# A chunked RWKV-7 recurrence and a GELU MLP in one kernel: the MLP moved one chunk later, and the start reordered

## The chip, the core and the metric

The kernel runs on one core of one Trainium2 chip. The metric is the device time of a whole execution in microseconds (us). TensorE (PE) multiplies matrices out of SBUF into PSUM; VectorE (DVE), ScalarE (ACT) and GpSimd (POOL) do the elementwise work; SyncE (SP) issues most transfers. Each engine runs its own instructions in the order in which the program lists them, and waits on semaphores for the others. PSUM holds four tiles of the kind `duo`, which is all that TensorE writes to.

## What is computed

Two stages: a linear recurrence with a state of 40 x 40 for each of 4 x 8 heads over 768 steps, and an MLP with exact GELU on its output.

```python
batch, n_heads, seq, head_dim = (4, 8, 768, 40)     # r, k, v, w, a, b: float32
n_tokens, d_model, d_ff = (3072, 320, 2048)         # moe_w_in, moe_w_out: float64
for t in range(S):
    y[:, :, t] = np.einsum('bhd,bhde->bhe', rt, state)
    Sa = np.einsum('bhde,bhe->bhd', state, at)
    state_decay = state * wt[:, :, None, :] - np.einsum('bhd,bhe->bhde', Sa, bt)
    state = state_decay + np.einsum('bhd,bhe->bhde', vt, kt)
x = y.transpose(0, 2, 1, 3).reshape(B * S, H * D)
h = x @ w_in
out = (0.5 * h * (1.0 + erf(h * inv_sqrt2))) @ w_out
```

The two weights come as float64. [...]

## The kernel before, in words

The sequence is cut into 12 chunks of 64 steps. Inside a chunk the recurrence becomes matrix products; only the state goes from chunk to chunk. For a chunk c these are the steps, each a function (names of tiles as in the profile):

- `sums(c)`: logarithm of `w_raw` on ScalarE, running sums `cum` on TensorE, exponentials on ScalarE. `turns_a(c)`: scaling by them (`nb` on VectorE, `ks` on GpSimd) and transposes to `wT`, `aT`, `nT`. `turns_b(c)`: transposes to `kT`, `vT`, `rT`.
- `make_N(c)`: the products `N` of a head's steps with each other, and their 32 x 32 blocks to DRAM (`N<-N`).
- `invert(c)`: the blocks come back with one block in each partition (`Nb<-N`), and 31 columns, two instructions each, invert the unit triangular blocks into `W`. VectorE does it for chunk 0, GpSimd for all others.
- `fetch_inverse(c)`: `W` to DRAM (`inv<-W`) and back as a matrix (`Tt<-inv`, `T2`). `corner(c)` transposes it on VectorE (`L`) and multiplies (`J`); `joined(c)` adds the missing quarter (`J2`, the second `J` of the profile).
- `make_RV`, `make_A`, `make_av`, `make_X`, `make_sa`, `make_saT`, `make_M`, `make_y2`, `make_QY`: the products that lead to the output and the new state. `X` needs the state of the chunk before, `sap` needs `Tt`, and `QY` comes last.
- `outputs(c)`: VectorE makes `xt` (the MLP's input) and the new state `st` out of `QY`. Parts of `xt` then move between partitions by ten small transfers, `xt<-xt`, five issued by SyncE and five by ScalarE.
- `mlp(c)`: a generator that yields after each piece: four pieces `ph` (`xt` by `w_in`, then GELU into `gt`) and four pieces `po` (`gt` by `w_out`), each a few us of TensorE. `os` takes the result out of PSUM, and SyncE writes it.

`fill()` emits the next piece of the oldest MLP that is queued. The loop over chunks emits, in iteration c, `make_N` and `invert` of chunk c+1, the state-dependent steps of chunk c with `fill()` in between, `outputs(c)`, and then queues `mlp(c)` and goes on with the other steps of chunks c+1 and c+2, with four more `fill()`. So the four `ph` pieces of chunk c follow its own `outputs(c)`, and the `po` pieces fall into iteration c+1.

The order on TensorE and SyncE is that of the code (`manual_schedule`); on VectorE, ScalarE and GpSimd a scheduler at build time chooses it. All of SyncE's transfers form one queue: one that waits holds those behind it. `a`, `v`, `r`, `xt`, `os`, `Nb`, `W`, `Tt` and `gt` have one buffer each.

The weights are converted (`to_float`, seven VectorE instructions for a tile) in the first two iterations: five tiles of `w_in` (`first_load`, `first_convert`), whose words pass through two halves of the unused `gt`, and sixteen tiles of `w_out` (`second_weights`), whose words pass through two buffers `wo_raw`.

Of the kernel before, what the change touches and what calls it, by code (L numbers as in the profile page):

```python
# [10 lines left out]
FP32 = mybir.dt.float32  # L11
# [5 lines left out]

HI_MIN = float(np.array(0x38100000, np.uint32).view(np.float32))
# [3 lines left out]
def kernel(  # L22
# [103 lines left out]
    def rows_of(src, c, g, e):  # L126
        return src[G * g + e, :, c * C:(c + 1) * C, :].rearrange("h t d -> t h d")

    def fetch(c, n, src, eng):
        t = work.tile([P, G, H, D], FP32, tag=n + "_raw", name=n + "_raw")  # L130
        for g in range(G):
            for e in range(2):
                eng.dma_start(out=t[half(e), g], in_=rows_of(src, c, g, e))  # L133
        raws[c, n] = t

    def fetch_padded(c, n, src, eng, placed):

        t = padded[n]()
        for g in range(G):
            for e in range(2):  # L140
                rows = rows_of(src, c, g, e)
                if placed:
                    for y in range(2):
                        eng.dma_start(out=t[half(e), g, y::2, :D], in_=rows[:, NP * y:NP * (y + 1)])  # L144
                else:
                    eng.dma_start(out=t[half(e), g, :, :D], in_=rows)
        raws[c, n] = t
# [7 lines left out]
    def load_kb(c):  # L155
        fetch(c, "k", k, nc.sync)
        fetch(c, "b", b, nc.sync)
# [7 lines left out]
    ctx.enter_context(tc.manual_schedule(engines={mybir.EngineType.PE, mybir.EngineType.SP}))  # L165
# [54 lines left out]
    def to_float(dst, words):  # L220


# [3 lines left out]
        top = work.tile([P, LW], UINT32, tag="top", name="top")[:, :n]  # L226
        low = work.tile([P, LW], UINT32, tag="low", name="low")[:, :n]
        nc.vector.tensor_scalar(low, hi, 3, 0x3FFFFFFF, ALU.logical_shift_left, ALU.bitwise_and)
        nc.vector.scalar_tensor_tensor(top, hi, 0xC0000000, low, ALU.bitwise_and, ALU.bitwise_or)
        top, low_f = top.bitcast(FP32), low.bitcast(FP32)  # L230
        nc.vector.tensor_scalar(low, hi, 0x7FFFFFFF, None, ALU.bitwise_and)
        nc.vector.scalar_tensor_tensor(top, low_f, HI_MIN, top, ALU.is_ge, ALU.mult)
        nc.vector.tensor_scalar(low, top.bitcast(UINT32), 0xFF800000, None, ALU.bitwise_and)
        nc.vector.scalar_tensor_tensor(low_f, lo, 2.0 ** -52, low_f, ALU.mult, ALU.mult)
        nc.vector.tensor_tensor(dst, top, low_f, ALU.add)  # L235

    first_raw, second_raw = {}, {}

    def first_load(kt):
# [10 lines left out]
    def first_convert(kt):  # L250
        if kt in first_raw:
            to_float(w_in_sb[:, kt], first_raw.pop(kt))

    def second_weights(lo_f, hi_f):
        wide = moe_w_out.dtype != FP32
        src = moe_w_out.bitcast(UINT32) if wide else moe_w_out
        for f in range(lo_f, hi_f):
            dst = w_out_sb[:, f]
            to = work.tile([P, 2 * DM], UINT32, tag="wo_raw", name="wo_raw", bufs=2) if wide else dst
            nc.sync.dma_start(out=to, in_=src[f * P:(f + 1) * P])  # L260
            if wide:
                to_float(dst, to)
# [50 lines left out]
    def turns_b(c):  # L313
        t = turned_in[c]
        kT = t["kT"] = side("kT", "kT", 1)
# [6 lines left out]
        nc.vector.tensor_copy(vT, flip(by_place(v_), "vT_ps"))  # L322
        rT = t["rT"] = side("rT", "rT", 2)
        nc.vector.tensor_copy(rT, flip(by_place(raws.pop((c, "r"))), "rT_ps"))
# [396 lines left out]
```

## Time and profile before

| | |
|---|---|
| median of 3 runs | 992.87 us (the runs: 991.69, 992.87, 995.45) |
| the profiled execution | 997.0 us, its span 995.3 us, mean granted TensorE clock 0.859 |
| busy: PE, PEld, DVE, ACT, POOL | 747.5, 609.4, 317.6, 236.5, 301.7 us |
| transfers | 60.41 MB in 255247 packets, mean 61 GB/s |
| in the first 50 us | 123 GB/s |

The span runs from the first to the last instruction. A row of the timeline gives start, length, engine, line, operation, output<-inputs, shapes, count, and in brackets the idle time ahead of it with what ended it. SPq and ACTq are the issues of transfers by SyncE and ScalarE. In a row of the groups the numbers behind the bar are busy us and mean ns of one instruction. TensorE takes a float32 product in two passes, so a count in the trace is twice that of the program.

### The profile page before, as it was taken

Reading aid. Unit: us, or ns where it says so; the run is one execution under the profiler, and the core shown is the slowest. Engines: PE = TensorE matmul, PEld = TensorE weight load, DVE = VectorE, ACT = ScalarE, POOL = GpSimd, SP = SyncE. Lnnn points to the kernel's source line nnn. Section 1 sums busy time; section 2 is a strip of 40 time slices with the busy share of each in tenths; the row PEclk is TensorE's granted clock in tenths of the full one; section 3 lists DMA queues with packets and bytes.
Section 4 is the critical chain, followed back from the end, with each engine's and each line's share of the span. In section 5 each row is a group of like instructions: output and inputs, shape, how many; then the busy total and the mean of one; then the engine's idle time right before and its main releaser. Section 6 shows DMA issues by size and latency. Waiting matters only on the chain.

```text
span 995.3 us, 29674 instructions
## 1 busy us (share of the span) xinstructions
PE 747.5 (75%) x13256; PEld 609.4 (61%) x13256; DVE 317.6 (32%) x479; ACT 236.5 (24%) x254; POOL 301.7 (30%) x777
## 2 busy tenths in 40 slices
PE   3433407667896994994995996995994996988978
PEld 2332406545774873874874874874874875867776
DVE  2771637783132132222231232221322322230110
ACT  2200013201511520520520611611511413302110
POOL 3008100008218118117036036036045054062000
PEclk9655658788898898997997997997997997998989
DMA  8624273345224134134143053043053053012000
GB/s 126 121 45 83 68 105 91 87 104 88 40 55 79 33 59 79 29 66 78 22 83 71 15 90 68 9 90 67 9 96 68 11 100 59 13 37 39 9 21 14
DMA packets 255247, 60.41 MB, mean 61 GB/s; under 512 B 241232, under 2 KB 250960, under 8 KB 255120
## 3 DMA queue, kind: packets, MB, share of 16 engines
q1 hardware_dynamic: 248864, 55.89, 30.6%
q10 hardware_dynamic: 6256, 2.63, 1.3%
q8 instruction: 104, 1.70, 0.7%
q14 instruction: 23, 0.19, 0.1%
HBM read 44.30 MB, written 10.22 MB: 55 GB/s over the span
## 4 chain that ended last, share of the span: by engine, by line
PE 64%; SPq 12%; DMA 10%; DVE 10%; issue 4%; POOL 0%; ACTq 0%; DVEq 0%; ACT 0%; POOLq 0%
PE ph L576 22%; PE po L583 19%; SPq L144 6%; DMA xt<-xt 3%; PE QY L98 2%; DMA out_dram<-os 2%; PE J L98 2%; SPq L133 2%; SPq L590 1%; PE saT_ps L98 1%; PE RV_ps L98 1%; PE cum L98 1%; PE A_ps L98 1%; PE M_ps L98 1%; PE kT_ps L284 1%
## 5 line engine op out<-in xcount | busy, mean ns | idle before, releaser
L576 PE MATMUL ph<-xt,w_in_sb 64*128 64x256 f32 x1920 | 246.5, 414 | 150.5 <-DMA xt<-xt 150.5
L576 PEld LDWEIGHTS ph<-xt,w_in_sb 64*128 64x128 f32 x1920 | 207.3, 207 | 182.4 <-issue 160.5
L583 PE MATMUL po<-w_out_sb,gt 128*128 128x320 f32 x768 | 224.7, 446 | 5.9 <-DVE w_out_sb L235 5.5
L398 POOL TENSOR_TENSOR tmp<-W,Nb 128x126 f32<-128x126 f32 (+22 forms) x341 | 125.1, 367 | 342.6 <-DMA Nb<-N 316.6
L583 PEld LDWEIGHTS po<-w_out_sb,gt 128*128 128x128 f32 x768 | 144.6, 193 | 65.6 <-DVE w_out_sb L235 6.5
L400 POOL TENSOR_TENSOR W<-W,tmp 128x126 f32<-128x126 f32 (+22 forms) x341 | 130.2, 382 | 26.7
L578 ACT ACTIVATE gt<-ph 128x1024 f32<-128x1024 f32 x48 | 49.2, 1024 | 187.9 <-PE ph L576 187.9
L578 ACT ACT_TABLE_LOAD x30 | 38.5, 1283 | 159.5 <-DMA xt<-xt 156.9
L304 POOL TENSOR_TENSOR ks<-k_raw,part 128x640 f32<-128x640 f32 x12 | 21.5, 1792 | 103.4 <-ACT part L276 103.4
L587 DVE COPY os<-po 128x320 f32<-128x320 f32 x24 | 11.8, 492 | 128.0 <-PE po L583 84.4
L494 ACT COPY saT<-saT_ps 128x512 f32<-128x512 f32 x12 | 7.0, 586 | 178.7 <-issue 157.6
L274 DVE COPY cs_pad<-cum 128x640 f32<-128x640 f32 x12 | 9.9, 823 | 114.7 <-PE cum L98 114.7
L533 DVE TENSOR_TENSOR y<-QY,y 128x512 f32<-128x512 f32 x22 | 15.1, 686 | 64.3 <-PE QY L98 64.3
L322 DVE COPY vT<-vT_ps 128x1024 f32<-128x1024 f32 x12 | 14.7, 1224 | 54.9 <-PE vT_ps L284 54.9
L98 PE MATMUL cum<-w_raw,cum_m 128*128 128x320 f32 x48 | 18.4, 512 | 16.6 <-ACT w_raw L269 16.6
L328 DVE TENSOR_TENSOR SM<-M_ps,upper 128x1024 f32<-128x1024 f32 x12 | 14.7, 1224 | 50.2 <-PE M_ps L98 50.2
L390 POOL MEMSET W<- 128x512 f32 x11 | 5.8, 529 | 82.0 <-DMA inv<-W 82.0
L328 DVE TENSOR_TENSOR VR<-RV_ps,upper 128x1024 f32<-128x1024 f32 x12 | 14.7, 1223 | 44.6 <-PE RV_ps L98 44.6
L455 DVE COPY Tt<-J 32x512 f32<-32x512 f32 x12 | 8.3, 689 | 59.4 <-ACT Tt L455 59.4
L284 PE MATMUL vT_ps<-ident,v_pad 128*128 128x128 f32 x96 | 14.5, 298 | 16.7 <-DMA v_pad<-in_v_dram 16.7
L308 DVE TENSOR_TENSOR aT<-aT_ps,wpT 128x1024 f32<-128x1024 f32 x12 | 14.7, 1224 | 33.7 <-ACT wpT L306 27.5
L269 ACT ACT_TABLE_LOAD x12 | 15.4, 1283 | 38.6 <-DMA w_raw<-in_w_dram 27.6
(110 smaller groups left out, 937.2 us busy)
## 6 DMA issues: line engine op xcount, KB each, us to landing
Nb<-N SPq DMA_DIRECT2D x24, 256.0 KB
wo_raw<-in_moe_w_out_dram SPq DMA_DIRECT2D x16, 320.0 KB
w_raw<-in_w_dram SPq DMA_DIRECT2D x48, 80.0 KB
k_raw<-in_k_dram SPq DMA_DIRECT2D x48, 80.0 KB
b_raw<-in_b_dram SPq DMA_DIRECT2D x48, 80.0 KB
r_pad<-in_r_dram SPq DMA_DIRECT2D x96, 40.0 KB
out_dram<-os SPq DMA_DIRECT2D x48, 80.0 KB
a_pad<-in_a_dram SPq DMA_DIRECT2D x44, 80.0 KB
```

Of the source, the lines that this page charges most:

```text
L98: nc.tensor.matmul(o, lhsT, rhs, start=first, stop=True, skip_group_check=True)
L133: eng.dma_start(out=t[half(e), g], in_=rows_of(src, c, g, e))
L144: eng.dma_start(out=t[half(e), g, y::2, :D], in_=rows[:, NP * y:NP * (y + 1)])
L269: nc.scalar.activation(logw, logw, ACT.Ln)
L284: nc.tensor.transpose(pt[:, g, n], src(g, n), ident)
L304: nc.gpsimd.tensor_tensor(ks[:, :, :, :D], raws.pop((c, "k")), rwv, ALU.mult)
L328: nc.vector.tensor_tensor(to, pt, upper.unsqueeze(1).to_broadcast([P, 2 * G * NP, C]), ALU.mult)
L398: eng.tensor_tensor(t, W[:, :rows, j:j + 1].to_broadcast([P, rows, rest]), Nb[:, j:j + 1, j + 1:].to_broadcast([P, rows, rest]), ALU.mult)
L400: eng.tensor_tensor(W[:, :rows, j + 1:], W[:, :rows, j + 1:], t, ALU.add)
L576: nc.tensor.matmul(ph[:, x, s], w_in_sb[half(x), kt, p * P:(p + 1) * P], xt[half(x), kt], start=kt == 0, stop=kt == NK - 1)
L578: nc.scalar.activation(gt[:, 4 * q:4 * q + 4].rearrange("p (s x) t -> p x s t", x=2), ph, ACT.Gelu)
L583: nc.tensor.matmul(po, gt[:, f, g * P:(g + 1) * P], w_out_sb[:, f], start=f == 0, stop=f == NF - 1)
```

## The change

1. **The MLP one chunk later.** Chunk 0 has an iteration of its own, written out, without any `fill()`. In the others the eight `fill()` stand as before, so they now emit the MLP of the chunk before: `ph` in the first half of the iteration, `po` behind `outputs`. `po` uses one PSUM tile for both halves of the tokens over four pieces.
2. **The order on VectorE and GpSimd** is that of the code too, and only ScalarE is left to the scheduler.
3. **Fewer transfers.** A half of the partitions now holds two neighbouring batches, so one transfer brings what took two; `N`, `Tt` and `T2` take half as many; all ten `xt` transfers of chunks 1 to 10 are issued by SyncE.
4. **Another conversion**, in pieces that are begun and finished apart: the exponent on ScalarE, five instructions on VectorE; the last two of them on GpSimd, with two more on ScalarE, for tiles 0 and 1 of `w_in`. Words of tiles 2 and 3 and of some `w_out` tiles pass through `w_out_sb`. The tiles of `w_out` are loaded behind chunk 1's inverse.
5. **The second inverse apart**: chunk 1's blocks and `W` have places of their own (`w_out_sb`, `wo_raw`) instead of the buffers of chunk 0's. Chunk 0's columns are emitted in three parts, between the steps of chunk 1.

```diff
     def rows_of(src, c, e):
+        return src[G * e:G * (e + 1), :, c * C:(c + 1) * C, :].rearrange("g h t d -> t (g h) d")
     def fetch(c, n, src, eng):
-        for g in range(G):
-            for e in range(2):
-                eng.dma_start(out=t[half(e), g], in_=rows_of(src, c, g, e))
+        for e in range(2):
+            eng.dma_start(out=t[half(e)].rearrange("p g h d -> p (g h) d"), in_=rows_of(src, c, e))
...
-    ctx.enter_context(tc.manual_schedule(engines={mybir.EngineType.PE, mybir.EngineType.SP}))
+    ctx.enter_context(tc.manual_schedule(engines={mybir.EngineType.PE, mybir.EngineType.SP,
+                                                 mybir.EngineType.DVE, mybir.EngineType.Pool}))
...
+    def to_float(dst, words, eng):
+        power = work.tile([P, LW // 2], UINT32, tag="power", name="power", bufs=2)[:, :n]
+        mant = work.tile([P, LW // 2], UINT32, tag="mant", name="mant", bufs=2)[:, :n]
+        nc.vector.tensor_scalar(power, hi, 0x7FF00000, None, ALU.bitwise_and)
+        nc.scalar.activation(power, power, ACT.Relu, bias=rebias, scale=8.0)
+        nc.vector.tensor_scalar(mant, hi, 0x000FFFFF, 0x00100000, ALU.bitwise_and, ALU.bitwise_or)
+        yield
+        nc.vector.scalar_tensor_tensor(power, hi, 0x80000000, power, ALU.bitwise_and, ALU.bitwise_or)
+        if eng is nc.vector:
+            eng.scalar_tensor_tensor(mant_f, lo, 2.0 ** -32, mant, ALU.mult, ALU.add)
+            eng.scalar_tensor_tensor(dst, mant_f, 2.0 ** -20, power_f, ALU.mult, ALU.mult)
+        else:
+            nc.scalar.mul(lo_f, lo, 2.0 ** -52)
+            nc.scalar.mul(mant_f, mant, 2.0 ** -20)
+            eng.tensor_tensor(mant_f, mant_f, lo_f, ALU.add)
+            eng.tensor_tensor(dst, mant_f, power_f, ALU.mult)
+        yield
+    def convert(n, last=False):
+        for _ in range(n):
+            begun.append(queue.pop(0))
+            next(begun[-1], None)
+            if len(begun) > 1:
+                next(begun.pop(0), None)
...
-            to = scratch[:, kt % 2 * 2 * LW:(kt % 2 + 1) * 2 * LW]
+            to = (late_raw if kt in (2, 3) else scratch)[:, kt % 2 * 2 * LW:(kt % 2 + 1) * 2 * LW]
...
-            eng = nc.scalar if x else nc.sync
+            eng = nc.scalar if x and c in (0, NCH - 1) else nc.sync
...
-        for g in range(G):
-            po = duo("po")[:, 0, :DM]
-            for f in range(NF):
-                nc.tensor.matmul(po, gt[:, f, g * P:(g + 1) * P], w_out_sb[:, f], start=f == 0, stop=f == NF - 1)
-                if f == NF // 2 - 1:
-                    yield
+        po = duo("po")[:, :, :DM]
+        for part in range(2):
+            for g in range(G):
+                for f in range(NF // 2 * part, NF // 2 * (part + 1)):
+                    nc.tensor.matmul(po[:, g], gt[:, f, g * P:(g + 1) * P], w_out_sb[:, f],
+                                     start=f == 0, stop=f == NF - 1)
+                if part:
+                    os = work.tile([P, DM], FP32, tag="os", name="os")
+                    nc.vector.tensor_copy(os, po[:, g])
...
+                yield
...
+        if c == 0:
+            load_w(2)
...
+            convert(1)
+            make_saT(0)
+            make_M(0)
+            make_QY(0, 0)
+            make_QY(0, 1)
+            outputs(0)
+            pieces.append(mlp(0))
+            turns_b(1)
...
+            fetch_inverse(1)
+            for f, place in (0, None), (1, None), (2, 14), (3, 12), (4, 10), (5, 8):
+                second_load(f, place)
...
+            continue
```

Three places show how it moves instructions. The first is TensorE behind `QY` of chunk 1. Before, the chunk's own `ph` follows:

```order
L98 MATMUL QY<-VR_120,ks_113 64x104 x32
L98 MATMUL QY<-SM_121,nb_117 64x104 x32
L576 MATMUL ph<-xt,w_in_sb 128x256 x20
L98 MATMUL av<-VR_119,A 64x40 x32
L98 MATMUL cum<-w_raw,cum_m 128x320 x2
```

Now it is `po` of chunk 0:

```order
L96 MATMUL QY<-VR_112,ks_105 64x104 x32
L96 MATMUL QY<-SM_113,nb_109 64x104 x32
L630 MATMUL po<-w_out_sb,gt 128x320 x8
L96 MATMUL av<-VR_111,A 64x40 x32
L96 MATMUL cum<-w_raw,cum_m 128x320 x2
```

What follows `QY` at once no longer reads that chunk's `xt`.

The second is VectorE between `cum` and the end of a steady chunk. Before, `L` comes ahead of `nb` and `aT`, and both `os` of the chunk lie outside this stretch:

```order
L274 COPY cs_pad_68<-cum 128x16x40
L431 STREAM_TRANSPOSE L<-Tt_122 128x512
L303 SCALAR_TENSOR_TENSOR nb_115<-b_raw,part_128 128x16x40
L308 TENSOR_TENSOR aT<-aT_ps,wpT_107 128x1024
L322 COPY vT<-vT_ps 128x1024
L324 COPY rT<-rT_ps 128x1024
```

Now `L` stands behind `os` of the third MLP piece:

```order
L314 COPY cs_pad_68<-cum 128x16x40
L343 SCALAR_TENSOR_TENSOR nb_107<-b_raw,part_120 128x16x40
L348 TENSOR_TENSOR aT<-aT_ps,wpT_99 128x1024
L634 COPY os<-po 128x320
L478 STREAM_TRANSPOSE L<-Tt_114 128x512
L363 COPY vT<-vT_ps 128x1024
L365 COPY rT<-rT_ps 128x1024
L634 COPY os<-po 128x320
```

`L` has moved behind a copy that needs the `po` piece which TensorE runs just ahead of `J`.

The third is SyncE's queue around `inv` of chunk 1. Before, the last `w_in` tile, all loads of chunk 2, `xt` of chunk 0 and eight `w_out` tiles are ahead of it:

```order
L144 DMA v_pad_70<-in_v_dram 64x4x40 x8
L144 DMA r_pad_72<-in_r_dram 64x4x40 x8
L540 DMA xt<-xt 24x1024
L543 DMA xt<-xt 16x256 x4
L260 DMA wo_raw<-in_moe_w_out_dram 128x640 x8
L409 DMA inv<-W 1024x1x32 x2
L417 DMA Tt_122<-inv 32x8x32 x2
```

Now the `w_out` tiles stand behind it, and `N` of chunk 2 behind six of them:

```order
L145 DMA v_pad_70<-in_v_dram 64x4x40 x8
L145 DMA r_pad_72<-in_r_dram 64x4x40 x8
L457 DMA inv<-wo_raw 1024x1x32 x2
L463 DMA Tt_114<-inv 32x16x32 x4
L467 DMA T_1162<-inv 32x8x32 x2
L291 DMA wo_raw<-in_moe_w_out_dram 128x640 x2
L291 DMA w_out_sb<-in_moe_w_out_dram 128x640 x4
L400 DMA N<-N 32x16x32 x4
L437 DMA Nb<-N 64x1024 x2
```

`inv` and `Tt` of chunk 1 have moved ahead of all `w_out` tiles.

More of the change, by code (lines that the diff above doesn't have):

```diff
@@ L138, in fetch_padded @@
         t = padded[n]()
-        for g in range(G):
[L140 to L146, printed above, removed]
+        for e in range(2):
+            rows = rows_of(src, c, e)
+            if not placed:
+                eng.dma_start(out=t[half(e)].rearrange("p g h d -> p (g h) d")[:, :, :D], in_=rows)
+                continue
+            for g in range(G):
+                for y in range(2):
+                    at = H * g + NP * y
+                    eng.dma_start(out=t[half(e), g, y::2, :D], in_=rows[:, at:at + NP])
         raws[c, n] = t
@@ L237 @@
+    queue, begun = [], []
+    def convert(n, last=False):
[4 more added lines that the diff above has]
+                next(begun.pop(0), None)
+        if last:
+            while begun:
+                next(begun.pop(0), None)
     first_raw, second_raw = {}, {}
+    late_raw = w_out_sb.rearrange("p f d -> p (f d)").bitcast(UINT32)
     def first_load(kt):
@@ L663 @@
         outputs(c)
[L664 to L666 removed]
+        seconds(2, (11, None), last=True)
         pieces.append(mlp(c))
@@ L677 @@
             turns_a(n + 1)
+        seconds(4, last=True)
         fill()
```

225 lines of the change are left out of this document (133 added, 92 removed).

## The prediction

> **What bounds the kernel now.** The page's chain of work that ended last is TensorE for 64%, then SyncE's queue, DMA and VectorE. The view of waits says where TensorE stands still: 150.5 us in 12 waits for one transfer, the `xt` copies that complete a chunk's MLP input.
>
> ```profile
> PE 64%; SPq 12%; DMA 10%; DVE 10%; issue 4%; POOL 0%; ACTq 0%; DVEq 0%; ACT 0%; POOLq 0%
> PE ph L576 <- DMA xt<-xt: 150.5, 12, 35.7
> ```
>
> The timeline of TensorE over one chunk (start, length, work, idle ahead of it) shows the shape that ten chunks share.
>
> ```profile
> 456.06 1.61 PE L98 MATMUL QY<-SM,nb 64*64 64x104 f32 x64
> 470.32 6.16 PE L576 MATMUL ph<-xt,w_in_sb 64*128 64x256 f32 x40 [12.65 <-DMA xt<-xt]
> 478.76 4.59 PE L576 MATMUL ph<-xt,w_in_sb 64*128 64x256 f32 x40
> 490.57 0.75 PE L98 MATMUL J<-L,N 32*32 32x32 f32 x64
> 500.09 1.16 PE L98 MATMUL N_ps<-aT,nT 40*64 40x64 f32 x64
> 527.85 1.61 PE L98 MATMUL QY<-SM,nb 64*64 64x104 f32 x64
> 541.55 4.72 PE L576 MATMUL ph<-xt,w_in_sb 64*128 64x256 f32 x24 [12.10 <-DMA xt<-xt]
> ```
>
> A chunk lasts 541.55 - 470.32 = 71.2 us: 59.1 of work, then 12.1 idle. Its first `ph` piece takes 6.16 instead of 4.59 us, and the row of the gap says why. In the rows of stretches the columns are the length, the busy time of PE, PEld, DVE, ACT and POOL, and then TensorE's granted clock: 0.58 in the gap, 1.00 later.
>
> ```profile
> 458.00:470.30 12.30, 0.00 (x0) 0.01 (x1) 3.92 (x8) 0.00 (x0) 10.26 (x27) 0.58 0.40 77
> 482.00:500.00 18.00, 18.00 (x278) 15.74 (x274) 5.72 (x5) 10.38 (x11) 1.46 (x1) 1.00 0.01 2
> 0.00:242.10 242.10, 118.90 (x2116) 97.20 (x2116) 134.00 (x251) 39.62 (x43) 53.44 (x142) 0.71 0.49 92
> 242.10:995.30 753.20, 628.57 (x11140) 512.21 (x11140) 183.55 (x229) 196.86 (x211) 248.26 (x635) 0.91 0.28 51
> ```
>
> So there are two stages with different limits. Up to 242.1 us (the end of chunk 1's `QY`) TensorE works 118.9 us and waits for loads and conversions; after it, 628.6 of 753.2 us, and waits for `xt`. The change is costed in each.
>
> **Steady chunks: the MLP one chunk later.** Behind `QY` of chunk c TensorE now has `po` of chunk c-1, whose `gt` is long finished. `xt` of chunk c is wanted only behind the next `X`, four MLP pieces and some 30 us later, against 12.1 us that it takes now. So the 12.1 us and the cold restart of 6.16 - 4.59 = 1.6 us go. Work per chunk, warm: 59.1 - 1.6 = 57.5 us.
>
> What is late next? VectorE's order is now written out, and in it `os`, the copy of the third MLP piece, stands ahead of `L`, the transpose for which `J` waits. TensorE runs that piece right ahead of `J`, so `J` waits for both. Before, `L` ran while TensorE was busy. These are the two, and the rows of the inverse's way from `N` to `L` (the last three from the chunk before).
>
> ```profile
> 465.64 0.49 DVE L587 COPY os<-po 128x320 f32<-128x320 f32 x1 [6.27 <-DMA out_dram<-os]
> 481.66 0.71 DVE L431 STREAM_TRANSPOSE L<-Tt 128x512 f32<-128x512 f32 x1 [1.97 <-DMA Tt<-inv]
> 501.76 1.23 DVE L328 TENSOR_TENSOR N<-N_ps,upper 128x1024 f32<-128x1024 f32 x1
> 503.01 3.76 SPq L360 DMA_DIRECT2D N<-N  x8
> 508.02 1.27 SPq L392 DMA_DIRECT2D Nb<-N  x2
> 512.88 0.24 POOL L398 TENSOR_TENSOR tmp<-W,Nb 128x31 f32<-128x31 f32 x1 [29.42 <-DMA Nb<-N]
> 540.94 0.23 POOL L400 TENSOR_TENSOR W<-W,tmp 128x16 f32<-128x16 f32 x1
> 471.12 1.28 SPq L409 DMA_DIRECT2D inv<-W  x2
> 474.49 0.81 SPq L417 DMA_DIRECT2D Tt<-inv  x2
> 479.87 0.87 SPq L417 DMA_DIRECT2D Tt<-inv  x2
> ```
>
> The new stall is 0.49 + 0.71 and 0.1 for the handing over, 1.3 us a chunk. Is the inverse itself in time? From the start of `N_ps`: 2.9 to the end of `N` (502.99 - 500.09). The issues of `N` halve from 3.76 to 1.9 and `Nb` follows 1.3 behind the last as before: 6.1. To GpSimd's first column 4.9 (512.88 - 508.02): 11.0. The columns take 28.3 (541.17 - 512.88): 39.3. From `inv` to the first `Tt` 3.4 (474.49 - 471.12): 42.7. Then four issues of `Tt` at 0.44, where twelve of `Tt` and `T2` took 6.7 us, and 1.5 to land (481.66 - 479.87 is 1.8 with two issues): 46. TensorE ends the third MLP piece 48 us after the start of `N_ps`: 29.4 to the end of `QY` (529.46 - 500.09) and what stands from `ph` to `J`, 490.57 - 470.32 = 20.2, less 1.6 cold. So the inverse has 2 us to spare.
>
> SyncE must be free for `inv` at 39. Its queue now issues all ten `xt` transfers, of which ScalarE had five; they can start at 31.5 and take about 6.6 (an estimate, at the 0.66 of a `v_pad` issue below): 38. The chunk's loads, 24 issues instead of 32, stand ahead of that and end near 24. A chunk thus comes to 57.5 + 1.3 = 58.8 us.
>
> Stalls of another kind stay. In four chunks TensorE stood still inside `X`, put down to "issue", and at one of these two the clock was lost too:
>
> ```profile
> PE X L98 <- issue: 5.4, 4, 1.7
> 284.71 0.66 PE L98 MATMUL X<-st,aT 40*64 40x40 f32 x28 [1.26 <-issue]
> 285.30 6.26 PE L583 MATMUL po<-w_out_sb,gt 128*128 128x320 f32 x16
> 648.62 0.25 PE L98 MATMUL X<-st,aT 40*64 40x40 f32 x1 [1.19 <-issue]
> 648.79 4.57 PE L583 MATMUL po<-w_out_sb,gt 128*128 128x320 f32 x16
> ```
>
> I keep them: 5.4 us, and two lost clocks by 6.26 - 4.57 = 1.7, 8.8 us. The same rows price the stall at `J` should it cost the clock: between 0 and 1.7 a chunk. I take 0, since 4.57 at 648.79 is the warm length although TensorE had stood for 1.19; the other end is a rival. The Trainium skill ("TensorE: Matmul & The Clock Gate", "What's actually happening") lets the clock halve only after an idle window of about 3.4 us. By that rule the stall at `J` never costs it; the row of 285.30, slow after 1.26 us, disagrees, so the rule doesn't remove the rival.
>
> **The start.** What sets the end of chunk 1's `QY` is the second inverse. GpSimd had it at 102.8; SyncE issued it only at 176.08.
>
> ```profile
> 102.57 0.23 POOL L400 TENSOR_TENSOR W<-W,tmp 128x16 f32<-128x16 f32 x1
> SPq L247 <- DVE xt L535: 19.3, 1, 19.3
> 137.17 5.25 SPq L144 DMA_DIRECT2D v_pad<-in_v_dram  x8
> 151.28 24.74 SPq L260 DMA_DIRECT2D wo_raw<-in_moe_w_out_dram  x8
> 176.08 1.31 SPq L409 DMA_DIRECT2D inv<-W  x2
> 187.39 1.08 PE L98 MATMUL J<-L,N 32*32 32x32 f32 x64 [8.33 <-DVE L L431]
> 240.47 1.61 PE L98 MATMUL QY<-SM,nb 64*64 64x104 f32 x64
> ```
>
> Now all tiles of `w_out` stand behind it (-24.74); the last `w_in` tile no longer waits for a buffer that VectorE frees late, since tiles 2 and 3 lie in `w_out_sb` (-19.3); and chunk 2's tensors need eight issues less, 8 by 5.25/8 (-5.3). 176.1 - 49.3 = 127. It can't be much below 103, where the columns end, nor do I see it above 176, where new waits on the queue replace the old. I take 127, because all three terms are rows of this queue.
>
> From `inv` to `J` 11.3 before (187.39 - 176.08), 8 with six issues for twelve. From `J` to the end of `QY`: 4.9 to `N_ps` (500.09 - 490.57 less a piece), then 29.4, and 3 for cold clocks, 37. So 127 + 8 + 37 = 172, between 148 and 221.
>
> The conversion had seven VectorE instructions a tile, four of 0.49 and three of 0.33 us. It has five there, and one on ScalarE; for the first two `w_in` tiles VectorE keeps three of half a tile, ScalarE has three and GpSimd two. The nearest rows for these are a ScalarE copy of 128x512 and GpSimd's product of 128x640:
>
> ```profile
> L229 DVE SCALAR_TENSOR_TENSOR top<-wo_raw,low 128x320 uint32<-128x320 uint32 x16 | 7.9, 492 | 0.6
> L228 DVE TENSOR_SCALAR low<-wo_raw 128x320 uint32<-128x320 uint32 x16 | 5.2, 327 | 19.6 <-DMA wo_raw<-in_moe_w_out_dram 19.2
> L494 ACT COPY saT<-saT_ps 128x512 f32<-128x512 f32 x12 | 7.0, 586 | 178.7 <-issue 157.6
> L304 POOL TENSOR_TENSOR ks<-k_raw,part 128x640 f32<-128x640 f32 x12 | 21.5, 1792 | 103.4 <-ACT part L276 103.4
> ```
>
> 2.13 us instead of 2.95 a `w_out` tile, 13 less for sixteen; ScalarE up to 0.59 an instruction; GpSimd eight by at most 1.79, 14 us, ahead of the second inverse. I cost all of it at nothing: VectorE works 134 of 242 us there, ScalarE 40, GpSimd 53. Without that cover it would be the 14 on GpSimd.
>
> What the fixed order costs is another thing: a conversion whose tile has not landed holds the attention steps behind it (`SM` of chunk 0 behind tile 3 of `w_in`). For chunks 0 and 1 that lies within the 172. It comes once more in chunk 1: `N` of chunk 2 is issued behind six `w_out` tiles (eight took 24.74, so 18.6), and `inv` of chunk 2 behind the last tiles, each of which waits for a conversion. An inverse with 2 us to spare then comes between 0 and 17 late; I add 10, since `po` needs the last tiles too.
>
> **The sum, from the profiled execution.** 172 + 10 to the end of chunk 1's `QY`; nine chunks by 58.8, 529; the tenth without a successor's sums, transposes and products, some 10 us less, 49; four pieces of `po` of chunk 10, 18 (done earlier before: moved, not saved); the last MLP, eight pieces, 37; the tail as now, 995.3 - 991.2 = 4.1; the small stalls, 8.8.
>
> ```profile
> 984.61 6.62 PE L583 MATMUL po<-w_out_sb,gt 128*128 128x320 f32 x24
> ```
>
> That is 828 of span. 1.7 us lie around it (997.0 - 995.3), so 830 against the profiled 997.0; the median of the runs, 992.87, is 0.4% below that one, hence 826.
>
> **Rivals.** (1) As summed: 826, its own range 800 to 850. (2) The clock falls at each stall at `J`: ten by 1.7, 843; the row of 285.30 speaks for it, that of 648.79 against. (3) The inverse binds: it has 2 us, and SyncE 1 us. A transfer of N, now twice as long, that lands 5 us later puts 3 to 5 us on ten chunks, 855 to 875. (4) The start doesn't shorten, because conversions in fixed order wait for tiles as SyncE's queue did: 242 for 172, 896. Against it: the tiles are issued tens of us earlier. (5) Slower: `po` is held over four pieces and keeps one of the four PSUM pairs (`duo`) from ten others between `QY` and `J2`. If each of the ten waited for the eviction of the third before it, TensorE would stand still ten times a chunk; from a mean wait of 1.7 us on the gain of 167 is gone, at 1.8 it is 1006. Against it: pieces of 4.59 us lie between the groups, and an eviction of 128x1024 takes 1.23. (6) The change doesn't do what it says, since `po` of the chunk before isn't ready either: the gap stays and the start alone gives 925. Only chunk 1 has that wait, for `w_out`.
>
> **How the numbers follow.** Chances: (1) 60%, (2) 13%, (3) 13%, (4) 8%, (5) 3%, (6) 3%. The range, 798 to 872, holds nearly all of (1) and (2) and most of (3), and leaves out (4) to (6). About 0.5% is what a measurement of this kernel can tell from no change. Faster by more: all but (5), 0.96; within it 0.01; slower 0.03.
>
> **What would show it.** Right: no `ph` waits for `xt` behind chunk 1; chunks of 58 to 60 us; `J` waits 1.2 to 1.4 us for `L`; chunk 1's `QY` ends near 172; a granted clock near 1.00 from there on. Wrong: `L` waits for `Tt` (3), `po` pieces of 6.2 us behind `J` (2), `wT` to `tn` waiting for evictions (5), `inv` of chunk 1 issued after 150 (4).

## The result: 848.2 us, 22 more than predicted and inside the range

The changed kernel takes 848.19 us (median of 4 runs, 846.30 to 850.00) against 994.16 for the one before (4 runs, 991.69 to 998.67): a ratio of 0.8527, 95% interval 0.8489 to 0.8565. The forecast was 826, from 798 to 872. The profiled execution took 848.96 us.

The page of the changed kernel: span, the engines' busy time, TensorE's clock in tenths over 40 slices, and the shares of the chain that ended last.

```profile
span 847.2 us, 29410 instructions
PE 724.1 (85%) x13256; PEld 592.3 (70%) x13256; DVE 291.1 (34%) x450; ACT 235.3 (28%) x271; POOL 320.3 (38%) x786
PEclk9555666988799999999999999999999999999999
PE 65%; DMA 9%; SPq 8%; DVE 7%; POOL 4%; issue 4%; ACT 2%; ACTq 0%; DVEq 0%; POOLq 0%
```

TensorE's work is what it was (13256 matmuls; 724 us for 748, at a mean granted clock of 0.919 for 0.859), and half of its idle time is gone (123 us for 248). In the row of the clock, 9 stands from the twelfth slice on, which is 90% or more. The same in stretches (length; busy PE, PEld, DVE, ACT, POOL; granted clock; DMA): to the end of chunk 1's `QY`, to that of chunk 2, eight chunks, the tenth interval, the end.

```profile
0.00:178.30 178.30, 94.19 (x2053) 82.08 (x2054) 85.83 (x168) 55.01 (x69) 65.05 (x147) 0.71 0.61 110
178.30:262.30 84.00, 68.48 (x1117) 52.09 (x1118) 40.92 (x77) 23.87 (x31) 31.82 (x78) 0.84 0.43 84
262.30:737.00 474.70, 459.20 (x8929) 379.47 (x8929) 150.23 (x185) 143.46 (x157) 216.04 (x544) 1.00 0.38 66
737.00:789.20 52.20, 49.35 (x873) 39.40 (x873) 10.04 (x16) 8.84 (x11) 7.42 (x20) 0.97 0.13 26
789.20:847.20 58.00, 52.84 (x288) 39.31 (x288) 4.06 (x8) 4.10 (x4) 0.00 (x0) 1.00 0.07 18
```

The eight chunks take 59.3 us each, at 1.00. Against the sum of the prediction these rows give: start 178.3 for 172 (+6.3); the stretch to chunk 2's `QY` 84.0 for 10 + 58.8 (+15.2); eight chunks 474.7 for 470.4 and the 8.8 of small stalls (-4.5); the tenth 52.2 for 49 (+3.2); the end 58.0 for 59.1 (-1.1). Together 847.2 for 828. One stretch holds most of the miss.

First the steady chunk, in TensorE's rows and then VectorE's:

```profile
436.62 1.61 PE L96 MATMUL QY<-SM,nb 64*64 64x104 f32 x64
438.15 4.57 PE L630 MATMUL po<-w_out_sb,gt 128*128 128x320 f32 x16
451.84 4.47 PE L630 MATMUL po<-w_out_sb,gt 128*128 128x320 f32 x16
457.60 0.74 PE L96 MATMUL J<-L,N 32*32 32x32 f32 x64 [1.29 <-DVE L L478]
458.28 1.09 PE L324 MATMUL kT_ps<-ident,ks 128*128 128x128 f32 x8
```

```profile
456.35 0.49 DVE L634 COPY os<-po 128x320 f32<-128x320 f32 x1 [3.77 <-PE po L630]
456.75 0.70 DVE L478 STREAM_TRANSPOSE L<-Tt 128x512 f32<-128x512 f32 x1
```

`po` of the chunk before starts as `QY` ends, where TensorE waited 12 us for `xt`. `J` waits 1.29 us for `os` and `L` one behind the other, and the transposes after it run at the warm 1.09 us.

Next the stretch that was mis-sized: the first five and the last of TensorE's seven waits for `w_out` in it, then `J` of chunk 2, and SyncE's issues of the last `w_out` tiles:

```profile
185.52 1.44 PE L630 MATMUL po<-w_out_sb,gt 128*128 128x320 f32 x2 [4.38 <-DVE w_out_sb L239]
188.11 1.43 PE L630 MATMUL po<-w_out_sb,gt 128*128 128x320 f32 x2 [1.15 <-DVE w_out_sb L239]
189.74 1.43 PE L630 MATMUL po<-w_out_sb,gt 128*128 128x320 f32 x2 [0.20 <-DVE w_out_sb L239]
206.01 0.81 PE L630 MATMUL po<-w_out_sb,gt 128*128 128x320 f32 x2 [0.16 <-DVE w_out_sb L239]
207.93 0.81 PE L630 MATMUL po<-w_out_sb,gt 128*128 128x320 f32 x2 [1.12 <-DVE w_out_sb L239]
...
215.03 2.77 PE L630 MATMUL po<-w_out_sb,gt 128*128 128x320 f32 x4 [3.12 <-DVE w_out_sb L239]
219.09 1.08 PE L96 MATMUL J<-L,N 32*32 32x32 f32 x64 [1.29 <-DVE L L478]
```

```profile
188.24 0.37 SPq L291 DMA_DIRECT2D wo_raw<-in_moe_w_out_dram  x1
196.74 0.52 SPq L291 DMA_DIRECT2D wo_raw<-in_moe_w_out_dram  x1
201.79 8.46 SPq L291 DMA_DIRECT2D wo_raw<-in_moe_w_out_dram  x3
```

`J` of chunk 2 comes at 219, 41 us behind `QY`; in a steady chunk it is 19 (457.60 against 438.23). The last tiles are issued from 201.8 to 210.3, when `po` already wants them. But not all waits are for late transfers. The count 2 of a `po` row is one tile, so the first three waits, 5.7 of 11.9 us, are for tiles 5 to 7, which SyncE had issued by 162.0; their conversions end at 185.5, 188.1 and 189.7, behind `outputs` in VectorE's written order. The stretch also costs clock: TensorE is busy for 68.5 us in it, at 0.84, where a chunk of the eight has 57.4 at 1.00. What holds the tiles back is the main question of the experiments.

### The profile page after: what moved, and what is told of

Same layout as the page of the kernel before. It is cut to its first block, busy times and chain, and to the rows that moved or that the text cites. A ratio compares the mean times of both kernels' runs of the same rounds, so it can differ in the third digit from the quotient of the medians.

```text
span 847.2 us, 29410 instructions
## 1 busy us (share of the span) xinstructions
PE 724.1 (85%) x13256; PEld 592.3 (70%) x13256; DVE 291.1 (34%) x450; ACT 235.3 (28%) x271; POOL 320.3 (38%) x786
## 4 chain that ended last, share of the span: by engine, by line
PE 65%; DMA 9%; SPq 8%; DVE 7%; POOL 4%; issue 4%; ACT 2%; ACTq 0%; DVEq 0%; POOLq 0%
PE po L630 21%; PE ph L622 21%; PE QY L96 3%; POOL W L447 2%; POOL tmp L445 2%; PE J L96 2%; SPq L145 2%; DMA Nb<-N 2%; DMA inv<-W 2%; PE kT_ps L324 2%; PE cum L96 1%; PE vT_ps L324 1%; PE tn_ps L324 1%; SPq L131 1%; SPq L589 1%
## 5 line engine op out<-in xcount | busy, mean ns | idle before, releaser
L630 PE MATMUL po<-w_out_sb,gt 128*128 128x320 f32 x768 | 222.9, 443 | 13.0 <-DVE w_out_sb L239 11.9
L445 POOL TENSOR_TENSOR tmp<-W,Nb 128x126 f32<-128x126 f32 (+22 forms) x310 | 115.2, 372 | 288.0 <-DMA Nb<-N 264.5
L622 PE MATMUL ph<-xt,w_in_sb 64*128 64x256 f32 x1920 | 222.4, 383 | 1.9 <-issue 1.0
L622 PEld LDWEIGHTS ph<-xt,w_in_sb 64*128 64x128 f32 x1920 | 183.4, 188 | 25.8 <-issue 2.4
L579 DVE TENSOR_TENSOR y<-QY,y 128x512 f32<-128x512 f32 x22 | 15.1, 686 | 69.0 <-PE QY L96 69.0
L96 PE MATMUL J<-L,N 32*32 32x32 f32 x768 | 9.9, 204 | 29.2 <-DVE L L478 29.2
L96 PE MATMUL QY<-SM,nb 64*64 64x104 f32 x768 | 20.7, 260 | 15.1 <-DVE SM L369 15.1
L232 ACT ACTIVATE power<-power,rebias 128x320 uint32<-128x320 uint32 (+1 forms) x26 | 16.1, 623 | 62.4 <-DVE power L231 62.4
L369 DVE TENSOR_TENSOR A<-A_ps,upper 128x1024 f32<-128x1024 f32 x12 | 14.7, 1225 | 54.1 <-PE A_ps L96 54.1
L369 DVE TENSOR_TENSOR VR<-RV_ps,upper 128x1024 f32<-128x1024 f32 x12 | 14.7, 1225 | 54.1 <-PE RV_ps L96 54.1
L369 DVE TENSOR_TENSOR SM<-M_ps,upper 128x1024 f32<-128x1024 f32 x12 | 14.7, 1224 | 54.1 <-PE M_ps L96 54.1
L96 PEld LDWEIGHTS J<-L,N 32*32 32x32 f32 x768 | 8.9, 116 | 34.8 <-issue 34.8
L96 PEld LDWEIGHTS cum<-w_raw,cum_m 128*128 128x128 f32 x48 | 10.1, 234 | 32.2 <-ACT w_raw L309 19.7
L96 PEld LDWEIGHTS QY<-SM,nb 64*64 64x64 f32 x768 | 19.1, 141 | 15.3 <-DVE SM L369 15.3
```

The lines of the kernel that those rows point to most:

```text
L96: nc.tensor.matmul(o, lhsT, rhs, start=first, stop=True, skip_group_check=True)
L232: nc.scalar.activation(power, power, ACT.Relu, bias=rebias, scale=8.0)
L369: nc.vector.tensor_tensor(to, pt, upper.unsqueeze(1).to_broadcast([P, 2 * G * NP, C]), ALU.mult)
L445: eng.tensor_tensor(t, W[:, :rows, j:j + 1].to_broadcast([P, rows, rest]), Nb[:, j:j + 1, j + 1:].to_broadcast([P, rows, rest]), ALU.mult)
L579: nc.vector.tensor_tensor(y2, Y, y2, ALU.add)
L622: nc.tensor.matmul(ph[:, x, s], w_in_sb[half(x), kt, p * P:(p + 1) * P], xt[half(x), kt], start=kt == 0, stop=kt == NK - 1)
```

## The experiments

Times are medians, ratios are against the kernel before on the same chip. The last three columns are read from the rows of `QY` in each trace: the end of chunk 1's `QY`, from there to that of chunk 2, and the mean of the eight chunks after it.

| kernel | us | ratio, 95% interval | `QY`(1) | to `QY`(2) | chunk |
|---|---|---|---|---|---|
| before | 994 to 998 | 1 | 242.1 | 72.3 | 72.2 |
| changed | 848.2 | 0.8527 (0.8489 to 0.8565) | 178.3 | 84.0 | 59.3 |
| lag undone | 971.7 | 0.9748 (0.9693 to 0.9804) | 179.8 | 98.5 | 73.2 |
| lag alone | 954.7 | 0.9579 (0.9533 to 0.9626) | 235.2 | 72.0 | 66.2 |
| `L` first | 839.6 | 0.8418 (0.8383 to 0.8454) | 177.9 | 83.9 | 58.4 |
| loads not merged | 856.3 | 0.8612 (0.8561 to 0.8664) | 185.9 | 88.2 | 59.2 |
| second inverse ahead | 847.8 | 0.8503 (0.8469 to 0.8536) | 175.9 | 85.6 | 59.3 |
| order by the scheduler | 840.9 | 0.8475 (0.8440 to 0.8510) | 177.1 | 77.8 | 59.3 |
| shared buffers | 848.7 | 0.8531 (0.8498 to 0.8565) | 181.1 | 83.7 | 59.6 |
| half of `w_out` | 839.7 | 0.8455 (0.8419 to 0.8491) | 183.6 | 69.7 | 59.7 |
| old conversion | 858.5 | 0.8660 (0.8621 to 0.8698) | 179.7 | 92.6 | 59.6 |
| queue of chunk 1 | 853.8 | 0.8568 (0.8531 to 0.8606) | 177.3 | 86.7 | 59.4 |
| all together | 833.0 | 0.8369 (0.8340 to 0.8398) | 168.0 | 87.4 | 58.6 |
| and tiles converted earlier | 825.0 | 0.8302 (0.8259 to 0.8345) | 169.3 | 81.2 | 58.5 |

### The lag undone, the rest kept

```diff
+        if c == 2:
+            fill(4)
         if more:
             make_N(n)
```

> The changed kernel with the lag alone undone from chunk 2 on: four MLP pieces more are emitted once, ahead of chunk 2's first product, so that the `ph` pieces of chunk c stand right behind its own `outputs(c)` again. Theory (the lag takes away 12.1 us of waiting for `xt` and 1.6 us of cold restart, and costs 1.3 us at `J`): each of ten chunks is 12.4 us longer, 848 + 124 = 972 us, and `ph` waits for `xt` ten times by some 12 us; with all ten `xt` issues on SyncE up to 3 us more a chunk, 1000 us. Rival (most of the steady gain comes from the merged transfers and the written order): the chunks stay under 64 us and the time under 910 us.

It took 971.7 us, and a chunk 73.2 for 59.3. TensorE's waits over the whole run, in us, times, longest:

```profile
PE ph L622 <- DMA xt<-xt: 104.3, 19, 10.5
```

The wait for `xt` is back, at 104 us for the 120 expected, and a chunk is 13.9 us longer for 12.4. The lag is worth some 123 us in this kernel; without it the other four parts save 2.5% together.

### The lag alone, in the kernel before

```diff
         pieces.append(mlp(c))
-        fill()
+        if c:
+            fill()
```

(and the same at the other three `fill()` behind it.)

> The kernel before with the lag alone: chunk 0 emits no MLP piece, everything else as it was (transfers not merged, VectorE and GpSimd ordered by the scheduler, the old start). Theory A (lag and start are independent): start 242 us, then nine chunks of 57.5, a tenth of 49, and 59 for the rest, with 9 us of small stalls, 877 us. Theory B (the lag needs the merged transfers, since 12 issues of `Tt` and `T2` where there are 6 and 8 of `N` where there are 4 make the inverse's way 53 us long against 48 us of other work): `J` waits about 5 us for `L` in each chunk, 920 us.

954.7 us: neither. B's mechanism is there, in TensorE's waits behind the start and in one chunk:

```profile
PE J L98 <- DVE L L431: 59.3, 10, 8.1
```

```profile
530.67 1.08 PE L98 MATMUL J<-L,N 32*32 32x32 f32 x64 [5.83 <-DVE L L431]
531.68 1.97 PE L284 MATMUL kT_ps<-ident,ks 128*128 128x128 f32 x8
```

`J` waits 5.9 us a chunk (B said 5), but B left out what such a wait does to the clock: `kT` behind it takes 1.97 for 1.09. A chunk comes to 66.2, not 62.5. So the two halves of the change do not add up. Alone they save 4.2% and 2.5%, which makes 6.7; together they save 14.7. Without the lag a shorter way for the inverse is worth little in a steady chunk; without the shorter way the lag runs into the inverse. That it is the merged transfers of `N`, `Tt` and `T2` that shorten the way was not run by itself: this kernel differs from the changed one also in its loads, its start and VectorE's order.

### `L` ahead of `os`

```diff
         seconds(4, last=True)
+        if more:
+            turn_corner(n)
         fill()
         if more:
             corner(n)
```

(`turn_corner` is the line of `corner` that transposes `Tt` into `L`.)

> The changed kernel with one thing moved: on VectorE the transpose `L` stands ahead of the copy `os` of the third MLP piece instead of behind it. Theory (the fixed order makes `J` wait 1.29 us in each steady chunk): ten times 1.2 us less, 836 us, and `J` no longer waits in most chunks. Rival (the inverse has no time to spare, `L` waits for `Tt` instead): 843 to 848 us.

839.6 us, 8.6 less, of the 12 expected. TensorE's waits for `L` behind 262 us fall from the first row (changed) to the second (this kernel):

```profile
PE J L96 <- DVE L L478: 13.7, 9, 2.9
```

```profile
PE J L96 <- DVE L L476: 5.9, 5, 1.7
```

In about half of the chunks `J` waits no more; in the others `L` waits for `Tt`, as the rival had it. So the order of two copies was worth 1.3 us a chunk only where the inverse was early enough.

### The loads in twice as many transfers

```diff
-        for e in range(2):
-            eng.dma_start(out=t[half(e)].rearrange("p g h d -> p (g h) d"), in_=rows_of(src, c, e))
+        for g in range(G):
+            for e in range(2):
+                eng.dma_start(out=t[half(e), g], in_=rows_of(src, c, e)[:, H * g:H * (g + 1)])
```

> The changed kernel with the loads of `w`, `k`, `b` and `a` in four transfers each instead of two: 32 issues a chunk for 24, by 0.66 us. Theory (SyncE has about 1 us to spare before `inv`): the ten `xt` issues and `inv` come 4 us later in eight chunks, `L` waits for `Tt`, and with the clock lost behind it each chunk is 4 to 6 us longer; the start 5 us: 885 to 900 us. Rival (the queue has room): 848 to 856 us.

856.3 us, at the upper end of the rival's range and 29 us short of the theory's. The steady chunk is 59.2 us, no longer than in the changed kernel; ahead of chunk 2's `QY` 11.9 us are lost, and some 3 come back behind it. A steady chunk, SyncE and then GpSimd:

```profile
454.95 0.84 SPq L588 DMA_DIRECT2D xt<-xt  x1
...
459.18 2.58 SPq L591 DMA_DIRECT2D xt<-xt  x4
462.49 1.30 SPq L459 DMA_DIRECT2D inv<-W  x2
```

```profile
462.24 0.23 POOL L449 TENSOR_TENSOR W<-W,tmp 128x16 f32<-128x16 f32 x1
```

The last `xt` issue ends at 461.8, the last column of the inverse at 462.5: the queue is free 0.7 us ahead. The merged loads were not issued at 0.66 us a transfer in the first place. `w`, `a`, `b` and `k` take 10.0 us in eight issues of the changed kernel (415.19 to 425.19) and 13.1 in sixteen here (489.83 to 502.92): 3 us more and not 5. And `xt` is no later for it: its first issue comes 2.3 us behind the end of `QY` here (454.95 against 452.65), and 2.2 in the changed kernel (381.30 against 379.09). There SyncE stood idle for 2.1 us between the last `r` and `xt` (438.63 to 440.69); here only 0.1 of it is left (454.83 to 454.95), so still more issues would have shown.

### The second inverse ahead of chunk 2's `v` and `r`

```diff
-            load_v(2)
-            load_r(2)
             sums(2)
             turn_state()
             fetch_inverse(1)
+            load_v(2)
+            load_r(2)
```

> The changed kernel with one thing moved in SyncE's queue: the second inverse (`inv` of chunk 1) is issued ahead of the 16 transfers of `v` and `r` of chunk 2 instead of behind them, 10.6 us earlier. Theory A (the loads and conversions of `w_out` set the end of chunk 1's MLP, and their place in the queue is the same): `QY` of chunk 1 ends up to 8.5 us earlier, `po` waits as much longer for `w_out`, the time stays within 3 us of 848. Theory B (the state's chain sets the start): 840 us.

847.8 us. `J` of chunk 1 comes 5.7 us earlier, and `QY` only 2.3:

```profile
133.50 0.74 PE L96 MATMUL J<-L,N 32*32 32x32 f32 x64 [1.30 <-DVE L L478]
141.47 0.63 PE L324 MATMUL rT_ps<-ident,r_pad 128*128 128x128 f32 x4 [1.92 <-DMA r_pad<-in_r_dram]
142.75 0.63 PE L324 MATMUL rT_ps<-ident,r_pad 128*128 128x128 f32 x4 [0.64 <-DMA r_pad<-in_r_dram]
```

`rT` now waits for the `r` that was moved behind. The time agrees with A, but the 2.3 us are too few to tell the theories apart: inconclusive on what sets the end, clear on the queue, where one transfer's gain is another's wait.

### VectorE and GpSimd ordered by the scheduler

```diff
-    ctx.enter_context(tc.manual_schedule(engines={mybir.EngineType.PE, mybir.EngineType.SP,
-                                                 mybir.EngineType.DVE, mybir.EngineType.Pool}))
+    ctx.enter_context(tc.manual_schedule(engines={mybir.EngineType.PE, mybir.EngineType.SP}))
```

> The changed kernel with VectorE and GpSimd ordered by the build-time scheduler, as before the change. The scheduler keeps `os` ahead of `L`, and puts `SM` of chunk 0 ahead of the conversion of `w_in` tile 3, which held it 15.1 us. Theory A (SyncE's queue sets the start, the hold lies beside it): `QY` of chunk 0 ends some 15 us earlier, and the time stays within 5 us of 848; `J` still waits 1.3 us a chunk. Theory B (the written order costs its 15 us): 833 us. Theory C (the written order is what brings the start forward): 870 us or more.

840.9 us, between A and B: 7 less by the medians, though the intervals of the two ratios touch (0.8440 to 0.8510, and 0.8489 to 0.8565). `SM` of chunk 0 runs at 88.47 instead of 101.06, `QY` of chunk 0 ends 12 us earlier, and `QY` of chunk 1 only 1.2: the hold of 15.1 us lay beside SyncE's queue, as A said. The gain came at another place, in the stretch to chunk 2's `QY` (77.8 for 84.0), because the scheduler also places the conversions of `w_out` differently: those of tiles 5 to 7 end ahead of chunk 1's `QY`, and the first `po` piece behind it, which in the changed kernel waits 5.7 us for them, runs through:

```profile
177.00 4.57 PE L629 MATMUL po<-w_out_sb,gt 128*128 128x320 f32 x16
```

So the written order costs some 6 us in that stretch, C is wrong, and the start is not brought forward by it.

### The second inverse in the buffers of the first

```diff
-    inverse = start_inverse(1, nc.gpsimd, (late_raw[:, 4 * LW:].bitcast(FP32), spare[0][:, :BL // 2 * BL], spare[1]))
-    run(inverse)
...
     fetch_inverse(0)
+    run(start_inverse(1, nc.gpsimd))
```

> The changed kernel with the second inverse in the same buffers as the first, so that it starts only when the first has been written out (some 76 us instead of 64). Theory (its result waits from 92 to 132 us in SyncE's queue): it ends near 110, still ahead of its issue, and the time stays within 4 us of 848. Rival (it is on the way to `J` of chunk 1): 858 us or more.

848.7 us. GpSimd's last column ends at 108.1 and SyncE issues the result at 134.9, so this part of the change is worth nothing that can be measured here.

### Half of `w_out`

```diff
-                    nc.tensor.matmul(po[:, g], gt[:, f, g * P:(g + 1) * P], w_out_sb[:, f],
+                    nc.tensor.matmul(po[:, g], gt[:, f, g * P:(g + 1) * P], w_out_sb[:, f % 8],
                                      start=f == 0, stop=f == NF - 1)
```

(and the loads and conversions of tiles 8 to 15 taken out.)

> Only the first eight of the sixteen `w_out` tiles are loaded and converted, and `po` uses each of them twice, so the output isn't the MLP's; TensorE's work is the same. Theory (in chunk 1 `po` waits for the late tiles, and that makes the stretch between the two `QY` 25 us longer than a steady chunk): the stretch falls from 83.9 to some 62 us and the time to 826. Rival (the inverse of chunk 2 or chunk 3's loads would hold the stretch anyway): 840 us or more.

839.7 us, at the rival's bound. The stretch falls to 69.7, not 62. Chunk 1's `QY` comes 5.3 us later: 1.4 of it are there at `QY` of chunk 0, and in chunk 1 `M` waits 1.85 us for `saT` and the clock falls behind that (`ph` in 5.67 us); why `saT` is late was not followed up. In the stretch, the late eight tiles therefore cost 14 of the 25 us by which it exceeds a steady chunk. Of the other 11, 4.9 is `po` waiting for tiles 5 and 6, whose conversions end behind `outputs` in VectorE's written order. The rest shows as a low clock: TensorE is busy for 62.3 us for 57.4, with `po` in 5.39 us and `av` in 1.95 where others take 4.47 and 1.14.

### The old conversion

```diff
+        if eng is nc.vector:
...
+            return
         power = work.tile([P, LW // 2], UINT32, tag="power", name="power", bufs=2)[:, :n]
```

(Left out are the seven instructions of the kernel before, with the first `yield` behind three of them.)

> The changed kernel with the old conversion (seven VectorE instructions, none on ScalarE) for the last three `w_in` tiles and all of `w_out`: 0.82 us more VectorE time a `w_out` tile, 13 us in all, and less waiting for ScalarE. Theory A (transfers set the catch-up, conversions are hidden): within 4 us of 848. Theory B (VectorE's work sets it): 855 to 861 us.

858.5 us: B. In the stretch behind chunk 1's `QY`, `po` waits for `w_out` as in the first row with the old conversion, and as in the second in the changed kernel:

```profile
PE po L645 <- DVE w_out_sb L241: 18.6, 8, 6.3
```

```profile
PE po L630 <- DVE w_out_sb L239: 11.9, 7, 4.4
```

(The conversion makes float32 of the float64 weights, which the kernel reads as pairs of 32-bit words.) The new one is worth 10 us, 8.6 of them in that stretch. Its price had been put at nothing because VectorE is idle half of the time there. But it lies in a loop: a buffer comes free when its tile is converted, and only then is the next transfer issued. SyncE's own waits in the changed kernel show it, where L291 issues the `w_out` tiles and `mant` is the last read of a tile's words:

```profile
SPq L291 <- DVE mant L238: 21.3, 7, 5.1
```

### Chunk 1's part of the queue

```diff
-            load_next(n + 1)
+            load_w(n + 1)
+            load_a(n + 1)
+            load_kb(n + 1)
...
         seconds(1, (10, None))
+        if c == 1:
+            load_v(n + 1)
...
         seconds(2, (12, 14), (13, None))
+        if c == 1:
+            load_r(n + 1)
```

(and half of chunk 1's `xt` issues on ScalarE.)

> The changed kernel with chunk 1's part of SyncE's queue reordered: `v` of chunk 3 behind `w_out` tile 10 and `r` of chunk 3 behind tile 13, and half of chunk 1's `xt` issues on ScalarE; nothing is left out. Theory (the late `w_out` tiles, eight to fifteen, are late because 16 transfers of `v` and `r` and ten of `xt` stand ahead of them): they land some 8 to 10 us earlier, the stretch from `QY` of chunk 1 to that of chunk 2 falls from 84 to 75 us, the time to 839. Rival (`v` and `r` are then late for chunk 3's transposes, or VectorE's conversions set the pace): 846 us or more.

853.8 us, no gain: the rival. (The profiled execution took 847.95, and its stretch is 86.7 us for 84.0.) SyncE and VectorE show why.

```profile
174.93 0.73 SPq L291 DMA_DIRECT2D w_out_sb<-in_moe_w_out_dram  x1
186.46 0.33 SPq L291 DMA_DIRECT2D wo_raw<-in_moe_w_out_dram  x1
```

```profile
185.81 0.62 DVE L238 SCALAR_TENSOR_TENSOR mant<-wo_raw,mant 128x320 f32<-128x320 uint32 x1
```

With `v` and `r` out of the way SyncE stands idle from 175.7 to 186.5 with tile 10 at its head, and issues it 0.03 us after VectorE's last read of tile 6 (185.81 + 0.62), which frees one of the two buffers. In the changed kernel the 16 transfers end at 187.5 and the buffer comes free at 187.5: two waits that ended together, so that the removal of one showed nothing.

### All together, and then the conversions earlier

The first of the two kernels joins `L` first, the second inverse ahead and chunk 1's queue with three moves of its own:

```diff
-            eng = nc.scalar if x and c in (0, NCH - 1) else nc.sync
+            eng = nc.scalar if x and c in (0, 1, NCH - 2, NCH - 1) else nc.sync
...
+    first_load(3)
     load_v(1)
     load_r(1)
-    first_load(3)
...
             make_sa(0)
-            convert(1)
             make_saT(0)
...
             outputs(0)
+            convert(1)
```

> The changed kernel with everything together that the runs point to: `L` ahead of `os`; chunk 1's queue as in the run above; half of the `xt` issues of chunk 10 on ScalarE; the conversion of `w_in` tile 3 behind `SM` and `outputs` of chunk 0; `w_in` tile 3 ahead of chunk 1's `v` and `r`, and the second inverse ahead of chunk 2's. Theory (the gains add: 8.6 for `L`, 7 for the hold of `SM`, 9 for the late tiles, 2 for chunk 10): 822 us. Rival (SyncE's queue and the transfers of the first 200 us hold the start whatever the order): 832 to 840 us.

833.0 us: in the rival's range, but not by its mechanism. `L` first gives what it gave, and the start is not held: `QY` of chunk 1 ends 10 us earlier (168.0). The stretch behind it grows to 87.4. The second kernel acts on the buffer:

```diff
-        seconds(1, (6, None))
+        seconds(2, (6, None))
         make_sa(c)
-        seconds(1, (7, None))
+        seconds(1, (7, None), (8, 14))
...
         make_M(c)
-        seconds(1, (9, 12))
+        seconds(2)
```

> The version before it (`L` first, the start's queue reordered), with the conversions of `w_out` in chunk 1 two and three places earlier in VectorE's order: tiles 0 to 7 stand ahead of `QY` of chunk 1 instead of 0 to 5. Theory (tile 10's transfer waits from 166 to 177 us for the buffer of tile 6, whose conversion stands behind `QY` and `outputs` in the written order, and all later tiles wait behind it): tile 10 is issued before `QY` ends, the stretch from `QY` of chunk 1 to that of chunk 2 falls from 87 to some 75 us, the time from 833 to 821. Rival (two buffers, each 3 us of transfer and 2 of conversion, and 16 transfers of `v` and `r` set the pace): 828 us or more.

825.0 us, with a stretch of 81.2. Tile 10, on SyncE, and the read that frees its buffer, on VectorE:

```profile
172.64 0.33 SPq L291 DMA_DIRECT2D wo_raw<-in_moe_w_out_dram  x1
```

```profile
171.94 0.67 DVE L238 SCALAR_TENSOR_TENSOR mant<-wo_raw,mant 128x320 f32<-128x320 uint32 x1
```

Tile 10 goes out 3.3 us behind the end of `QY` instead of 8.6, still right behind the read that frees the buffer: the theory's cause holds, but half of its gain. `po` still waits 10.0 us for `w_out` there. 6.2 of them are for tile 7: only tiles 0 to 6 end ahead of `outputs`, and the last three instructions of tile 7's conversion run behind it, to 180.2. For the tiles after that, whether two buffers or the queue sets the pace was not separated. This is the fastest version: 0.8302 of the kernel before, 23 us less than the changed one, and only that of the version before it touches its interval.

## Why the prediction was right, and where it was off

- **Steady chunks** (57.5 of work, 1.3 at `J`): right. 59.3 us with the small stalls in it, where 58.8 and 8.8 for all of these make 59.9; the stall at `J` is 1.29 us in seven of the eight chunks, by the mechanism given. The lag undone brought `xt` back at once.
- **Inverse with 2 us to spare**: right by a hair, and smaller than said. In one of the eight chunks it is late and `J` waits 1.84. With `L` first, `L` waits for `Tt` in every chunk, and `J` for that in about half, by up to 1.69 us, so in those there is little or nothing to spare. In the tenth `J` waits 2.85: there the ten `xt` issues end at 746.95 and `inv` follows at 747.06, later than the inverse itself, and the tenth is 3.2 us longer than forecast. The slack of 1 us on SyncE was near the 0.7 seen, though loads and queue came to it in another way than by 0.66 us an issue.
- **Clock at `J` free** (the choice of 0 between 0 and 1.7): right for every stall of 1.29 us. The other end does exist: it came with the stalls of 1.84 and 2.85.
- **Small stalls, 8.8**: too high. TensorE stood 3.1 us in `X` behind 262 us, with the clock kept.
- **Start 172**: 178.3. The three terms of the queue moved `inv` from 176.1 to 132.1, where 127 was predicted, and from `J` to the end of `QY` it is 39 for 37. The three were not separated: SyncE still stands 12.7 us in two waits with `w_in` tiles at its head, where the sum took all 19.3 out. And the second inverse no longer sets that end by itself: issued 10 us earlier, it moves `QY` by 2.3, and `rT` then waits for `r`. That conversions hold attention steps in the fixed order happened (`SM` of chunk 0 by 15.1 us) and lay within the start, as said.
- **Catch-up 10, between 0 and 17**: the step that failed; it was 25. The sum priced it as a late inverse of chunk 2, by the issues of six tiles ahead of its `N` (18.6 us). The six take 2.8 us to issue in the changed kernel (138.46 to 141.29), since each finds a free place, and the inverse isn't late: `J` of chunk 2 waits its usual 1.29. What the runs show in its place is `po` waiting 11.9 us for tiles. 5.7 of them are for tiles 5 to 7, whose conversions end behind `QY` and `outputs` in VectorE's written order; 6.1 are for later tiles, which go round a loop: transfer into one of two buffers, wait for a conversion, next transfer. Another 11 us are TensorE's work at a clock of 0.84. **Conversion at nothing** failed with it: +10 us with the old one.

Of the rivals, (2) and (3) showed in one or two chunks each; of (4) only 6 us; of (5) no row, since no product between `QY` and `J2` waits for an eviction of `po`; (6) only in chunk 1, where `po` waits for `w_out`.

## What to carry to other kernels

Where an engine idles, look at what would be late next before summing the gain: the lag alone was worth 4% and the rest alone 2.5%, and together they gave 15, because each half removed the wait that the other ran into (`xt` without the lag, the inverse with the lag alone). Work that is "hidden" has no price only if nothing waits for its result or its buffer: look at its place in its engine's order, and follow the buffer from the conversion back to the transfer that refills it. If a wait is removed and nothing happens, look for a second one that ends at the same moment.

## What the runs showed of the chip

The clock does not depend on the length of a stall alone. In the changed kernel a stall of 1.84 us at `J` cost it, and with `L` first one of 1.68 did not, while in that kernel 1.15 us in `X` did. With half of `w_out` a stall of 1.90 us at `J` kept it, and with the loads not merged one of 2.91. The changed kernel, then the one with `L` first:

```profile
635.36 0.74 PE L96 MATMUL J<-L,N 32*32 32x32 f32 x64 [1.84 <-DVE L L478]
636.04 1.96 PE L324 MATMUL kT_ps<-ident,ks 128*128 128x128 f32 x8
```

```profile
629.34 0.74 PE L96 MATMUL J<-L,N 32*32 32x32 f32 x64 [1.68 <-DVE L L476]
630.01 1.09 PE L324 MATMUL kT_ps<-ident,ks 128*128 128x128 f32 x8
...
699.45 0.78 PE L96 MATMUL X<-st,aT 40*64 40x40 f32 x37 [1.15 <-issue]
700.16 6.28 PE L626 MATMUL ph<-xt,w_in_sb 64*128 64x256 f32 x40
```

The Trainium skill ("TensorE: Matmul & The Clock Gate", "What's actually happening") says that the clock follows an activity window of some 3.4 us, which is free-running. Stalls of like length with unlike outcomes agree with that; a clock lost after 1.15 us of standing does not fit its rule that a whole window must be idle. No run here shows where the window stands.

GpSimd's columns take longer while VectorE makes `xt`. GpSimd, and then VectorE in the changed kernel:

```profile
437.82 0.44 POOL L447 TENSOR_TENSOR W<-W,tmp 128x120 f32<-128x120 f32 x1
438.83 0.74 POOL L447 TENSOR_TENSOR W<-W,tmp 128x121 f32<-128x121 f32 x1
```

```profile
438.36 0.94 DVE L581 TENSOR_TENSOR xt<-y,wpT 128x512 f32<-128x512 f32 x1
439.93 0.69 DVE L581 TENSOR_TENSOR xt<-y,wpT 128x512 f32<-128x512 f32 x1
```

GpSimd loses 0.3 us where they overlap, and VectorE 0.25 in the first of its two products and nothing in the second. Two such products fall into the inverse in each of these chunks; in all 20 of them, from chunk 1 to chunk 10, the GpSimd instruction that begins inside one takes 0.72 to 0.87 us, where others of that size take some 0.4. The Trainium skill ("SBUF — State Buffer", "SBUF: two separate sides") gives a cause, a port pair that the two engines hold in turn when VectorE reads two inputs from SBUF. The longer GpSimd rows agree with it; no run here took it apart.
